# A sparse matmul on one core: one activation tile is loaded on its own, one transposing load is split in two, and a few products change places

## The chip, the cores and the metric

The kernel runs on one NeuronCore of a Trainium2 chip. The metric is the device time of one execution in microseconds (us), lower is better. The time before is 233.01 us, the median of 3 runs that lie between 232.99 and 233.06 us.

## The reference

The weights `w` (1024 x 1024) are pruned 2:4 along the rows: of each four neighbouring rows, per column, the two values with the largest magnitude stay and the others become zero. Then the activations are multiplied by them and a bias is added.

```python
B, S, D = 16, 512, 1024            # bf16 throughout
mag   = jnp.abs(w.reshape(D // 4, 4, D))
order = jnp.argsort(mag, 1)
thr   = jnp.take_along_axis(mag, order[:, 2:3, :], 1)     # the second largest of each four
wp    = (w.reshape(D // 4, 4, D) * (mag >= thr)).reshape(D, D)
return jnp.einsum("bsd,df->bsf", x, wp) + b
```

## The kernel before, in words

The 8192 tokens are 64 tiles of 128 rows. TensorE (PE) computes, for each tile, eight contraction steps of 128 against 1024 output columns in two halves of 512 (h = 0, 1). The weights arrive in two groups of 512 rows (g = 0, 1), and pruning them takes time, so the kernel has a head in which PE works on what is ready already.

**Pieces.** The weights are pruned in six pieces (line 129): pieces 0 to 3 are the four 256-column strips of group 0, pieces 4 and 5 the two 512-column halves of group 1. VectorE (DVE) takes the magnitudes (`abs`), the larger and smaller of each pair (`hi`, `lo`), the threshold (`t1`, `t2`, `thr`), compares (`mask`) and multiplies (`mult`). Each piece has four weight rows of a group, m = 0 to 3, with the letters u, v, s, t; x means u and v together, y means s and t together. The tables `halves` and `part` say in which parts a piece is masked and multiplied, so that a product may begin when its part is there.

**The first seven tiles of x** (0 to 6) are loaded in natural layout, only their first 512 columns (`load_x`, line 102). SyncE (SP) and ScalarE (ACT) each issue loads on a queue of their own. PE transposes these tiles (token `T6a`: four 128x128 transposes of tile 6, line 194), ACT copies the result to SBUF (`C6a`, line 199), and `M6.0t` is the product of tile 6 with row t of piece 0 (128x256, line 224, one matmul; x and y are two). ACT stages finished sums (`S`, `U`, line 259).

**The packed weights** of group 0 and 1 are also copied into natural row order (`spread`, tokens `W0.0`, `W0.1`, `W1.0p`, `W1.0q`, `W1.1`; four copies of 128 KB each, p and q are the first and last two of the four). `W1.0q` is issued by ACT, the rest by SP.

**Tiles 6 to 11** also come by transposing loads into one buffer, `xlead`: `load_lead(0)` at line 128 loads the first 512 columns of tiles 7 to 11, token `X1` (line 354) the last 512 columns of tiles 6 to 11 in a single transposing load. Tokens `Y1` and `Y0` are transposing loads of the last 512 columns of tiles 3 to 5 and 0 to 2 into `xlow` (line 232).

**Products in natural order.** `E0`, `E1` open tile 7 and `A0h0` to `A3h1` open tiles 8 to 11 with the first four contraction steps (line 237). After that the list `closes` gives the last four steps of each half: (8,0), (9,0), (10,0), (11,0), (7,0), (6,0), (3,0), (4,0), (5,0), then (8,1) and so on. They read `xlead`, `xlow` and group 1 of the natural weights; the first one needs all four copies of `W1.0`, (8,1) those of `W1.1`. After the closes, batches of 4 and 8 tiles are loaded whole by transposing loads (`load_nat`, line 396) and multiplied in the same way.

**Order.** The dictionary `order` gives the order of the instructions of PE, DVE, ACT and SP by hand; every engine runs its list strictly in order. `needs` gives the dependencies between tokens, the framework puts the waits in.

Of the kernel before, what the change touches and what calls it, by code (L numbers as in the profile page):

```python
# [10 lines left out]
def kernel(  # L11
# [7 lines left out]
    nc = tc.nc  # L19
    P = 128  # L20
# [14 lines left out]
    HK = D // G  # L35
    assert G == 2 and Dout == 2 * FH and HK == 512
    xf = x.flatten_outer_dims()
    of = out.flatten_outer_dims()

    NPK = 7  # L40
    LEAD = 5
    STG = 8
    SOLO = 6
# [4 lines left out]
    t0 = NPK + LEAD  # L48
# [17 lines left out]
    def seq(eng, inst):  # L66
        if eng in tails:
            tc.add_manual_dep(inst.ins, tails[eng].ins.name, NOSYNC, reason="program order")
        tails[eng] = inst
        return inst  # L70
# [7 lines left out]
    def act(i):  # L78
        return seq("act", i)

    def sp(i):
        return seq("sp", i)
# [12 lines left out]
    def issue(eng, out_, in_):  # L95
        q = nc.sync if eng == "sp" else nc.scalar
        return seq(eng, q.dma_start(out_, in_))  # L97

    def load_w(g, c0, c1, ma=0, mb=4, eng="sp"):
        issue(eng, w_sb[:, g, ma:mb, c0:c1], wv[:, g, ma:mb, c0:c1])  # L100

    def load_x(ta, tb, eng="sp"):
        xs = const.tile([P, tb - ta, HK], bf16, name=f"x_{ta}")
        issue(eng, xs[:], xf[ta * P:tb * P, :HK].rearrange("(t p) k -> p t k", p=P))
        for t in range(ta, tb):
            x_sb[t] = xs[:, t - ta, :]

    xlead = const.tile([P, KT, (LEAD + 1) * P], bf16)

    def load_lead(g):  # L110
        t0 = NPK - g
        sp(nc.sync.dma_start_transpose(out=xlead[:, 4 * g:4 * g + 4, (t0 - SOLO) * P:],
                                       in_=xf[t0 * P:(NPK + LEAD) * P, g * HK:(g + 1) * HK]))
        return {t: xlead[:, :, (t - SOLO) * P:(t - SOLO + 1) * P] for t in range(t0, NPK + LEAD)}

    xnat, held = {}, {}

# [1 line left out]
    load_w(0, 0, 256, 2, 4, "act")  # L119
    load_x(SOLO, SOLO + 1, "act")  # L120
    act(nc.scalar.activation(spark[:], nc.const_aps.tensor(1.0, [P, 1], bf16), Act.Abs))
    load_x(3, 6)
    load_w(0, 256, 512)
    load_x(0, 3)
    load_w(0, 512, 768)
# [9 lines left out]
    def filler(n, rep=1):  # L135
        for _ in range(n):
            pe(nc.tensor.matmul(warm_ps[:, :rep * P], lhsT=nc.const_aps.tensor(1.0, [P, P], bf16),  # L137
                                rhs=nc.const_aps.tensor(1.0, [P, rep * P], bf16), start=True, stop=True))
# [4 lines left out]
    def spread(g, c0, c1, ks=range(4), eng="sp"):  # L143
        for k in ks:
            issue(eng, wp_nat[:, 4 * g + k, c0:c1], wp[32 * k:32 * k + 32, g, :, c0:c1])
# [43 lines left out]
    def transpose(t):  # L189
        xg = x_sb[t].rearrange("p (q m) -> p m q", m=4)  # L190
        bank = psum_o.tile([P, FH], fp32, name="ps") if t in OWN else psum_t.tile([P, FH], fp32, name="tp")
        tp = bank[:].bitcast(bf16)[:, :FH].rearrange("p (m q) -> p m q", m=4)
        for m in range(4):
            pe(nc.tensor.transpose(tp[:, m, :], xg[:, m, :], ident[:]))  # L194
        xpk[t] = tp

    def copy_xt(t):
        xt = xtp.tile([P, 4, P], bf16, name="xt")
        act(nc.scalar.copy(xt[:].bitcast(fp32), xpk[t].bitcast(fp32)))
        xpk[t] = xt  # L200
# [9 lines left out]
    def mm_piece(t, i, ms):  # L210
        g, c0, c1 = pieces[i]
        q, n = pair_of[t], c0 // CW
        if t == SOLO:
            key, d = (t, "h", c0 // FH), -(c0 // FH) * FH
        else:
            key, d = (q, n), pairs[q].index(t) * CW - n * CW
        new = key not in ps_open
        if new:
            ps_open[key] = psum_o.tile([P, FH], fp32, name="ps")
            left[key] = 8  # L220
        ps = ps_open[key]
        for m in range(ms.start, ms.stop):
            left[key] -= 1
            pe(nc.tensor.matmul(ps[:, c0 + d:c1 + d], lhsT=xpk[t][:, m, :],  # L224
                                rhs=wp[:, g, m, c0:c1],
                                start=(new and m == ms.start), stop=(left[key] == 0),
                                skip_group_check=True))

    def load_low(u):
        a, b_ = GROUPS[u]  # L230
        xlow = const.tile([P, 4, (b_ - a) * P], bf16, name=f"xlow{u}")
        sp(nc.sync.dma_start_transpose(out=xlow[:], in_=xf[a * P:b_ * P, HK:]))
        return {a + t: xlow[:, :, t * P:(t + 1) * P] for t in range(b_ - a)}
# [6 lines left out]
    def open_solo(h):  # L240
        ps = ps_open[(NPK, "h", h)] = psum_t.tile([P, FH], fp32, name="tp")
        nat(xnat[NPK], ps[:], h * FH, (h + 1) * FH, 0, 4, last=3)

    def open_nat(j, h):
        t = STG + j
        if j < 3:
            held[(t, h)] = psum_o.tile([P, FH], fp32, name="ps")
        else:
            held[(t, h)] = psum_t.tile([P, FH], fp32, name="tp")
        nat(xnat[t], held[(t, h)][:], h * FH, (h + 1) * FH, 0, 4)  # L250
# [3 lines left out]
    def stage(key):  # L254
        solo = key[1] == "h"
        q, h, at = (pair_of[key[0]], key[2], int(key[0] != SOLO)) if solo else (key[0], key[1] // 2, key[1] % 2)
        if (q, h) not in staged:
            staged[(q, h)] = stg.tile([P, 2, 2, CW], fp32, name="st")
        act(nc.scalar.copy(staged[(q, h)][:, at, :, :].rearrange("p t c -> p (t c)"), ps_open.pop(key)[:]))  # L259

    order = {
# [7 lines left out]
        ),  # L269
        "dve": (  # L270
# [4 lines left out]
        ),  # L275
        "act": (
            "C6a C5a C3a C4a S0b0 C2a C0a C1a abs2 S3b0 S2b0 abs3 S0b1 U6h0 S3b1 S2b1 S0b2 S3b2 S2b2 S0b3 U6h1 "
            "S3b3 S2b3 U7h0 W1.0q U7h1"
        ),
        "sp": (  # L280
            "W0.0 Z W0.1 X1 W1.0p Y1 Y0 W1.1"
        ),
    }
    written = {"X0"}
    p = {}
    halves = {0: tuple("uvst"), 1: ('s', 't', 'x'), 2: ('s', 't', 'x'), 3: ('x', 'y')}

    by_rows = {0}

# [3 lines left out]
    def split_tok(tok):  # L293
        k = tok[-1] if tok[-1] in "xyabuvst" else ""
        return (tok[:-1] if k else tok), k
# [43 lines left out]
    def emit(eng, tok):  # L339
        base, k = split_tok(tok)  # L340
        if tok[0] == "T":
            transpose(int(tok[1:-1]))
            if int(tok[1:-1]) not in OWN:
                transposed.append(tok[1:])
        elif tok[0] == "F":
            filler(int(tok[1:]))
        elif tok[0] == "W":
            g, h = map(int, tok[1:4].split("."))
            spread(g, h * FH, (h + 1) * FH, {"": range(4), "p": range(2), "q": range(2, 4)}[tok[4:]], eng)
        elif tok[0] == "Z":  # L350
            load_w(1, 512, 1024)
            sp(nc.sync.dma_start(bias_sb[:], b.partition_broadcast(P)))
        elif tok[0] == "X":
            xnat.update(load_lead(int(tok[1:])))
        elif tok[0] == "Y":
            xnat.update(load_low(int(tok[1:])))
        elif tok[0] == "E":
            open_solo(int(tok[1:]))
        elif tok[0] == "U":
            t, h = map(int, tok[1:].split("h"))  # L360
            stage((t, "h", h))
        elif tok[0] == "A":
            open_nat(*map(int, tok[1:].split("h")))
        elif tok[0] == "C":
            copy_xt(int(tok[1:-1]))
        elif tok[0] == "M":
            mm_piece(*map(int, base[1:].split(".")), part[k])
        elif tok[0] == "S":
            stage(tuple(map(int, tok[1:].split("b"))))
        else:  # L370
            i = int(base[-1])
            if i not in p:
                p[i] = Piece(i)
            if eng == "act":
                p[i].abs_act()
            else:
                p[i].do(base[:-1], part[k], half.get(k, slice(0, 2)))
# [79 lines left out]
    for bi, (tb, nb) in enumerate(batches):  # L457
        if bi:
            load_batch(bi + 1)
        for j in range(nb):  # L460
            t = tb + j
# [49 lines left out]
```

## Time and profile before

| | |
|---|---|
| median of 3 runs | 233.01 us |
| the profiled execution, its own time | 233.04 us |
| its span, first to last instruction | 231.2 us |
| PE busy | 226.9 us (98%), 1144 matmuls |
| DVE busy | 107.7 us (47%) |
| ACT busy | 14.0 us (6%) |
| POOL busy | 17.6 us (8%) |
| granted TensorE clock over the span | 1.000 |

Times in the rows of the profile count from the start of the span. A row of the timeline has the start in us, the time from its start to the end of the last of its instructions, the engine, the line and operation, the tiles, and how many instructions were merged. Matmuls are pipelined, so one begins before the one ahead has ended: a product of 128x256 lasts 0.27 us by its row, and the next begins 0.109 us after it. SPq and ACTq are the instructions by which SP and ACT issue transfers. A row of the issues has the size in KB and the time from issue to landing.

### The profile page before, as it was taken

The page shows a single profiled execution, that of the slowest core. Times are in us where ns is not written, and L with a number is a line of the kernel's source. Part 1 is how long each engine was busy: PE and PEld are TensorE (multiplying, and loading weights), DVE is VectorE, ACT ScalarE, POOL GpSimd, SP SyncE. Part 2 cuts the span into 40 slices and gives each one's busy share as a digit, 9 for nine tenths or more (in the row PEclk, how much of TensorE's full clock was granted, in tenths as well). Part 3 has the DMA queues.
Part 4 walks back from the last instruction along what each step waited for, and adds up shares of the span by engine and source line. Part 5 has one row for each costly group of instructions (what it writes and reads, how often), then busy time and mean ns, then how long its engine had stood idle before and what let it go on. Part 6 is the DMA issues. An engine that isn't in the chain of part 4 may idle for free.

```text
span 231.2 us, 2827 instructions
## 1 busy us (share of the span) xinstructions
PE 226.9 (98%) x1144; PEld 109.8 (47%) x1144; DVE 107.7 (47%) x194; ACT 14.0 (6%) x27; POOL 17.6 (8%) x15
## 2 busy tenths in 40 slices
PE   7999999999999999999999999999999999999995
PEld 4886444444444444444444444444444444444443
DVE  4999777844424424424424423423423433433434
ACT  2874100000000000000000000000000000000000
POOL 1000299700000000000000000000000000000000
PEclk9999999999999999999999999999999999999999
DMA  6999999997499222991259822797129932122122
GB/s 212 257 200 264 226 191 222 224 323 252 180 218 272 100 94 76 240 274 64 74 124 233 233 91 78 164 208 224 59 91 201 249 140 92 47 91 91 58 81 91
DMA packets 79260, 38.19 MB, mean 165 GB/s; under 512 B 64144, under 2 KB 71696, under 8 KB 79248
## 3 DMA queue, kind: packets, MB, share of 16 engines
q1 hardware_dynamic: 68464, 20.88, 45.8%
q10 hardware_dynamic: 10784, 17.14, 21.3%
q8 instruction: 9, 0.15, 0.3%
q14 instruction: 3, 0.02, 0.0%
HBM read 3.28 MB, written 16.78 MB: 87 GB/s over the span
## 4 chain that ended last, share of the span: by engine, by line
PE 97%; DMA 2%; ACTq 0%; DVE 0%; issue 0%
PE ps L237 88%; PE ps L224 5%; PE tp L237 2%; DMA x<-in_x_dram 2%; PE tp L194 1%; PE ps L194 0%; ACTq L97 0%; DVE o L422 0%
## 5 line engine op out<-in xcount | busy, mean ns | idle before, releaser
L237 PE MATMUL ps<-wp_nat,xb 128*128 128x512 bf16 (+2 forms) x848 | 179.8, 375 | 0.0
L237 PEld LDWEIGHTS <-xb 128*128 128x128 bf16 x848 | 82.4, 98 | 97.5
L422 DVE TENSOR_TENSOR o<-ps,bias_sb 128x512 bf16<-128x512 f32 (+1 forms) x112 | 71.6, 677 | 113.6 <-PE ps L237 113.5
L418 POOL TENSOR_TENSOR st<-st,bias_sb 128x1024 f32<-128x1024 f32 x8 | 16.7, 2125 | 0.0
L237 PE MATMUL ps<-wp_nat,xlead 128*128 128x512 bf16 x64 | 14.9, 379 | 0.0
L237 PEld LDWEIGHTS <-xlead 128*128 128x128 bf16 x88 | 8.6, 98 | 10.3 <-issue 0.3
L224 PE MATMUL ps<-wp,xt 128*128 128x256 bf16 x112 | 12.8, 273 | 0.0
L424 DVE TENSOR_TENSOR o<-ps,st 128x512 bf16<-128x512 f32 x16 | 11.0, 691 | 3.3 <-PE ps L237 2.0
L224 PEld LDWEIGHTS <-xt 128*128 128x128 bf16 x112 | 10.6, 98 | 1.5
L237 PE MATMUL ps<-wp_nat,xlow 128*128 128x512 bf16 x48 | 10.7, 379 | 0.0
L259 ACT COPY st<-ps 128x512 f32<-128x512 f32 x14 | 7.4, 596 | 3.3 <-PE ps L224 3.2
L237 PEld LDWEIGHTS <-xlow 128*128 128x128 bf16 x48 | 4.7, 98 | 5.7
L158 DVE TENSOR_TENSOR mag<-mag,hi 128x256 bf16<-128x256 bf16 (+2 forms) x14 | 6.0, 459 | 0.2
L158 DVE TENSOR_TENSOR wp<-w_sb,mag 128x256 bf16<-128x256 bf16 (+2 forms) x14 | 6.0, 457 | 0.1
L237 PE MATMUL tp<-wp_nat,xlead 128*128 128x512 bf16 x24 | 6.0, 379 | 0.0
L137 PE MATMUL ps<-const-bfloat16-1.0 128*128 128x128 bf16 (+1 forms) x20 | 3.6, 351 | 0.8 <-PEq L495 0.8
L168 DVE TENSOR_SCALAR mag<-w_sb 128x512 uint16<-128x512 uint16 (+2 forms) x5 | 2.3, 476 | 3.3 <-DMA w_sb<-in_w_dram 3.3
L158 DVE TENSOR_TENSOR hi<-mag 128x512 bf16<-128x512 bf16 (+2 forms) x7 | 3.2, 458 | 0.1
L158 DVE TENSOR_TENSOR lo<-mag 128x512 bf16<-128x512 bf16 (+1 forms) x6 | 3.1, 509 | 0.0
L137 PEld LDWEIGHTS <-const-bfloat16-1.0 128*128 128x128 bf16 x20 | 1.8, 118 | 2.4 <-issue 2.4
L194 PEld LDWEIGHTS <-x 128*128 128x128 bf16 x28 | 1.9, 115 | 1.0 <-DMA x<-in_x_dram 0.9
L194 PE MATMUL tp<-ident,x 128*128 128x128 bf16 x16 | 1.5, 223 | 0.8 <-DMA x<-in_x_dram 0.8
(18 smaller groups left out, 16.8 us busy)
## 6 DMA issues: line engine op xcount, KB each, us to landing
out_dram<-o ACTq DMA_DIRECT2D x58, 256.0 KB, 2.4
wp_nat<-wp SPq DMA_DIRECT2D x14, 128.0 KB, 3.7
out_dram<-o ACTq DMA_DIRECT2D x10, 128.0 KB, 1.7
w_sb<-in_w_dram SPq DMA_DIRECT2D x2, 512.0 KB, 5.7
x<-in_x_dram SPq DMA_DIRECT2D x2, 384.0 KB, 4.6
w_sb<-in_w_dram SPq DMA_DIRECT2D x3, 256.0 KB, 5.1
bias_sb<-in_b_dram SPq DMA_DIRECT2D x1, 256.0 KB, 4.5
wp_nat<-wp ACTq DMA_DIRECT2D x2, 128.0 KB, 3.4
```

Of the source, the lines that this page charges most:

```text
L137: pe(nc.tensor.matmul(warm_ps[:, :rep * P], lhsT=nc.const_aps.tensor(1.0, [P, P], bf16), rhs=nc.const_aps.tensor(1.0, [P, rep * P], bf16), ...
L158: dve(nc.vector.tensor_tensor(out, a, b_, op=op))
L168: dve(nc.vector.tensor_single_scalar(self.mag[:, ms, :].bitcast(u16), self.w[:, ms, :].bitcast(u16), 0x7FFF, op=Alu.bitwise_and))
L194: pe(nc.tensor.transpose(tp[:, m, :], xg[:, m, :], ident[:]))
L224: pe(nc.tensor.matmul(ps[:, c0 + d:c1 + d], lhsT=xpk[t][:, m, :], rhs=wp[:, g, m, c0:c1], start=(new and m == ms.start), stop=(left[key] = ...
L237: pe(nc.tensor.matmul(ps, lhsT=xt[:, kt - koff, :], rhs=wp_nat[:, kt, c0:c1], start=(kt == first), stop=(kt == last)))
L259: act(nc.scalar.copy(staged[(q, h)][:, at, :, :].rearrange("p t c -> p (t c)"), ps_open.pop(key)[:]))
L418: pool(nc.gpsimd.tensor_tensor(st[:], st[:], bias.to_broadcast([P, 2, 2, CW]), op=Alu.add))
L422: dve(nc.vector.tensor_tensor(o[:, c0:c1], ps, bias_sb[:, c0:c1], op=Alu.add))
L424: dve(nc.vector.tensor_tensor(o[:, c0:c1].rearrange("p (n c) -> p n c", n=2), ps.rearrange("p (n c) -> p n c", n=2), add, op=Alu.add))
```

## The change

Four things are altered, all of them in the head of the kernel:

- The load of tiles 3, 4 and 5 on SP's queue becomes two: tile 5 alone first, then tiles 3 and 4.
- The second transposing load into `xlead`, tiles 6 to 11, becomes two: `X1` loads tiles 8 to 11, and `X2`, behind `W1.0p` on SP, loads tiles 6 and 7.
- On PE, `M6.0s` trades places with `M5.0t`.
- Piece 3 is masked and multiplied by t, s and x, as pieces 1 and 2 are, in place of x and y, on DVE and in PE's products alike. DVE has six instructions for it where it had four; PE has the same matmuls in another order.

In the changed kernel the transposing loads into `xlead` stand on line 111 in place of 112, lines 123 to 268 keep their numbers, and lines from 270 on are higher by one.

```diff
-    def load_lead(g):
-        t0 = NPK - g
-        sp(nc.sync.dma_start_transpose(out=xlead[:, 4 * g:4 * g + 4, (t0 - SOLO) * P:],
-                                       in_=xf[t0 * P:(NPK + LEAD) * P, g * HK:(g + 1) * HK]))
-        return {t: xlead[:, :, (t - SOLO) * P:(t - SOLO + 1) * P] for t in range(t0, NPK + LEAD)}
+    def load_lead(g, ta=NPK, tb=NPK + LEAD):
+        sp(nc.sync.dma_start_transpose(out=xlead[:, 4 * g:4 * g + 4, (ta - SOLO) * P:(tb - SOLO) * P],
+                                       in_=xf[ta * P:tb * P, g * HK:(g + 1) * HK]))
+        return {t: xlead[:, :, (t - SOLO) * P:(t - SOLO + 1) * P] for t in range(ta, tb)}
...
-    load_x(3, 6)
+    load_x(5, 6)
+    load_x(3, 5)
...
         "pe": (
-            "T6a T5a T3a T4a M6.0t M5.0t M6.0s M5.0s M3.0t ..."
+            "T6a T5a T3a T4a M6.0t M6.0s M5.0t M5.0s M3.0t ..."
...
-            "... M3.3x M4.3x M6.3x M5.3x M2.3x M0.3x M1.3x M3.3y M4.3y M6.3y M5.3y M2.3y M0.3y M1.3y E0 ..."
+            "... M3.3t M4.3t M6.3t M5.3t M2.3t M0.3t M1.3t M3.3s M4.3s M6.3s M5.3s M2.3s M0.3s M1.3s "
+            "M3.3x M4.3x M6.3x M5.3x M2.3x M0.3x M1.3x E0 ..."
...
         "dve": (
-            "... hi3 lo3 t13 t23 thr3 mask3x mask3y mult3x mult3y abs4 ..."
+            "... hi3 lo3 t13 t23 thr3 mask3t mask3s mult3t mask3x mult3s mult3x abs4 ..."
...
         "sp": (
-            "W0.0 Z W0.1 X1 W1.0p Y1 Y0 W1.1"
+            "W0.0 Z W0.1 X1 W1.0p X2 Y1 Y0 W1.1"
...
-    halves = {0: tuple("uvst"), 1: ('s', 't', 'x'), 2: ('s', 't', 'x'), 3: ('x', 'y')}
+    halves = {0: tuple("uvst"), 1: ('s', 't', 'x'), 2: ('s', 't', 'x'), 3: ('s', 't', 'x')}
...
         elif tok[0] == "X":
-            xnat.update(load_lead(int(tok[1:])))
+            xnat.update(load_lead(1, *((STG, NPK + LEAD) if tok == "X1" else (SOLO, STG))))
```

11 rows, old and new, of the table order are left out of this document.

## The prediction

> **What bounds the kernel now.** I read the page first, for the share of PE, then the chain of waits, for the places where PE doesn't run on without a break.
>
> ```profile
> PE 226.9 (98%) x1144; PEld 109.8 (47%) x1144; DVE 107.7 (47%) x194; ACT 14.0 (6%) x27; POOL 17.6 (8%) x15
> ```
>
> ```profile
> 1.27 3.85 DMA x<-in_x_dram
> ```
>
> ```profile
> 5.16 0.74 PE tp L194 x8
> 5.90 0.45 PE ps L194 x8
> ```
>
> ```profile
> 24.53 2.59 PE ps L237 x12
> ```
>
> ```profile
> 27.98 2.72 PE ps L237 x12
> ```
>
> The chain waits for a load of x until 5.11 and is on PE from 5.16 to the end. So only time that PE loses can be won, and the change touches nothing behind the last product from `xlow`, at 48.5 by a row below. After 5.16 the losses are small: twelve matmuls take 2.59 us in one place and 2.72 us from 27.98, so 0.13 us is lost there. The timeline of PE, looked at in narrow windows, shows that place and two more.
>
> ```profile
> 5.16 0.41 PE L194 MATMUL tp<-ident,x 128*128 128x128 bf16 x4 [0.77 <-DMA x<-in_x_dram]
> ```
>
> ```profile
> 5.48 0.41 PE L194 MATMUL tp<-ident,x 128*128 128x128 bf16 x4
> ```
>
> ```profile
> 6.18 0.47 PE L224 MATMUL ps<-wp,xt 128*128 128x256 bf16 x2
> ```
>
> ```profile
> 6.37 0.50 PE L224 MATMUL ps<-wp,xt 128*128 128x256 bf16 x3
> ```
>
> ```profile
> 27.82 0.73 PE L237 MATMUL ps<-wp_nat,xlead 128*128 128x512 bf16 x2
> ```
>
> T6a's four transposes begin at 5.16 and T5a's at 5.48. The last eight transposes, from 5.90, take 0.45 us, 0.056 each, so T5a could begin at 5.38, or 5.41 with some 0.03 for starting after a wait: 0.07 us lost, and 0.03 more for T5a's own start. M6.0t begins at 6.18 and the next product at 6.37, where products step by 0.11 (the three from 6.37 to 6.87 last 0.27 each): 0.08 lost. At 27.82 two matmuls take 0.73 us; one lasts 0.38 (a row below has 379 ns), so the second began at 28.17, 0.35 behind the first in place of 0.22: the 0.13 again. All of it is some 0.3 us. **That is the ceiling of this change**, 0.13% of the span.
>
> **The head, part by part.** What arrives when is told by the issues and their times to landing, one stretch each.
>
> ```profile
> x<-in_x_dram SPq DMA_DIRECT2D x1, 384.0 KB, 4.2
> w_sb<-in_w_dram SPq DMA_DIRECT2D x1, 256.0 KB, 4.5
> x<-in_x_dram ACTq DMA_DIRECT2D x1, 128.0 KB, 3.8
> ```
>
> ```profile
> x<-in_x_dram SPq DMA_DIRECT2D x1, 384.0 KB, 4.9
> ```
>
> ```profile
> 1.24 0.46 SPq L97 DMA_DIRECT2D x<-in_x_dram  x1
> 1.75 0.68 SPq L97 DMA_DIRECT2D w_sb<-in_w_dram  x1
> 2.47 0.61 SPq L97 DMA_DIRECT2D x<-in_x_dram  x1
> ```
>
> ```profile
> 5.20 6.44 SPq L112 DMA_TRANSPOSE xlead<-in_x_dram  x1
> ```
>
> ```profile
> 19.17 4.02 SPq L112 DMA_TRANSPOSE xlead<-in_x_dram  x1
> ```
>
> Tile 6, on ACT's queue, lands at 1.27 + 3.8 = 5.1 and starts PE; nothing of the change moves it forward. Tiles 3 to 5 land at 1.24 + 4.2 = 5.44, piece 1's weights at 1.75 + 4.5 = 6.25, tiles 0 to 2 at 2.47 + 4.9 = 7.4. *Tile 5 alone* is a third of that load, of tile 6's size and issued at the same 1.24, so it should land with tile 6 or before it; I take no wait at T5a. Tiles 3 and 4 are issued 0.51 us later, which is the step from one SP issue to the next (1.24 to 1.75), and so is all that follows on SP up to `load_lead(0)`. These landings are paced by bytes, though: 256 KB lands 0.81 us behind the 384 KB, the next 384 KB 1.1 us behind that, 320 to 350 KB each us, while each had been issued over 3 us before the one ahead of it had landed. An issue later by 0.51 still comes before its turn, so the landings stay: 5.44 for tiles 3 and 4, wanted by T3a at 5.16 + 8 x 0.056 + 0.03 = 5.64. I cost the added issue at nothing; without that cover it is 0.51 us on each load, which is the second rival.
>
> PE then ends the sixteen transposes at 5.16 + 16 x 0.056 + 0.03 = 6.08, not 6.18. Now the products want their operands.
>
> ```profile
> 5.93 0.38 ACT L199 COPY xt<-tp 128x256 f32<-128x256 f32 x1
> ```
>
> ```profile
> 5.93 0.28 DVE L158 TENSOR_TENSOR wp<-w_sb,mag 128x256 bf16<-128x256 bf16 x1
> ```
>
> C5a ends at 5.93 + 0.38 = 6.31 and the product behind it starts at 6.37: 0.06 us from end to use. `mult0s` ends at 5.93 + 0.28 = 6.21, `mult0t` one step of DVE ahead of it; DVE's work isn't touched there. So M6.0t may begin at 6.08, *M6.0s* (in M5.0t's place) at 6.21 + 0.06 = 6.27, and the third product, M5.0t, at 6.38; C5a, started by its transposes 0.05 earlier, is done by then. In before the third product begins at 6.37 + 0.11 = 6.48. **The head gains 0.10 us**, not the sum of its gaps, since `mult0s` is late next. T2a follows 0.10 earlier too:
>
> ```profile
> 7.80 0.39 PE L194 MATMUL tp<-ident,x 128*128 128x128 bf16 x4
> ```
>
> That is 7.70, with its first weights loaded 0.1 before; tiles 0 to 2 have landed by 7.4.
>
> *Piece 3 by t, s, x.* Two rows of before, one of each form, give its price.
>
> ```profile
> 14.93 0.76 DVE L158 TENSOR_TENSOR mag<-mag,hi 128x512 bf16<-128x512 bf16 x2
> 15.60 0.76 DVE L158 TENSOR_TENSOR wp<-w_sb,mag 128x512 bf16<-128x512 bf16 x2
> 16.27 0.69 DVE L168 TENSOR_SCALAR mag<-w_sb 128x2048 uint16<-128x2048 uint16 x1
> ```
>
> ```profile
> 11.92 0.49 DVE L158 TENSOR_TENSOR mag<-mag,hi 128x256 bf16<-128x256 bf16 x2
> ```
>
> ```profile
> 13.41 0.42 DVE L158 TENSOR_TENSOR hi<-mag 128x512 bf16<-128x512 bf16 x1
> ```
>
> ```profile
> 15.91 0.49 PE L224 MATMUL ps<-wp,xt 128*128 128x256 bf16 x3
> ```
>
> The old form lasts 16.27 - 14.93 = 1.34 us, the new one, as piece 2 has it, 13.41 - 11.92 = 1.49. DVE is later by 0.15 from there on. Piece 3's first product is the last of the row from 15.91 (15.91 + 2 x 0.11 = 16.13); its `mult3x` ended at 15.60 + 0.42 = 16.02, so with PE 0.10 earlier it would have just been waited for, some 0.05. In the new form `mult3t` is done at about 15.6, `mult3s` is wanted 0.76 later, x at 17.6, and all are there. It wins nothing now, and keeps what the head won.
>
> **The split of X1.** What PE waited for at 27.82 isn't named by the view of waits. The second matmul of that stretch needs the second copy of `W1.0p`:
>
> ```profile
> 23.96 0.89 SPq L97 DMA_DIRECT2D wp_nat<-wp  x1
> ```
>
> ```profile
> wp_nat<-wp SPq DMA_DIRECT2D x1, 128.0 KB, 4.2
> xlow<-in_x_dram SPq DMA_TRANSPOSE x1, 5.1
> ```
>
> ```profile
> 20.84 1.22 DVE L158 TENSOR_TENSOR wp<-w_sb,mag 128x2048 bf16<-128x2048 bf16 x1
> ```
>
> It lands at 23.96 + 4.2 = 28.16, and the matmul starts at 28.17. Its issue stood behind `X1`, which held SP from 19.17 for 4.02 us, while its weights (`mult4`) were done at 22.06. With four of six tiles `X1` holds SP for an estimated 4.02 x 4/6 = 2.7 us, to 21.85, or 22.35 if the 0.51 of the head is still there; `mult4`, later by 0.15, ends at 22.21. So `W1.0p` is issued about 0.9 to 1.1 us earlier, lands near 27.1, and PE, 0.10 earlier, wants it at 27.94. **0.13 us goes**, with 0.8 to spare. `X1` itself, shorter, lands before its 19.17 + 6.6 = 25.8 of now.
>
> `X2` is put behind, and its price on SP is estimated from the next rows: `Y1` holds SP for 1.81 us with 3 tiles, so 2 tiles are 1.2 us.
>
> ```profile
> xlead<-in_x_dram SPq DMA_TRANSPOSE x1, 6.6
> ```
>
> ```profile
> 24.90 1.81 SPq L232 DMA_TRANSPOSE xlow<-in_x_dram  x1
> ```
>
> ```profile
> wp_nat<-wp SPq DMA_DIRECT2D x1, 128.0 KB, 3.6
> ```
>
> ```profile
> 31.02 1.33 SPq L97 DMA_DIRECT2D wp_nat<-wp  x1
> ```
>
> ```profile
> L237 PE MATMUL ps<-wp_nat,xlow x48: 379/379/379, 33.1 to 48.5; 128*128 128x512 bf16 x48
> ```
>
> ```profile
> 35.73 1.46 PE L237 MATMUL ps<-wp_nat,xlead 128*128 128x512 bf16 x6
> ```
>
> Tile 7 is wanted at 27.82 + 16 x 0.216 + 0.13 = 31.4; `X2`, issued near 24.0 and landing in the 5.1 to 6.6 us of its kind, is there by 30.6 at worst. What is queued behind it is `Y1`, `Y0` and `W1.1`. `W1.1`'s last copy was issued at 31.02 and landed 3.6 later at 34.65; its first user is the fourth matmul from 35.73, at 36.38: 1.7 us of slack. The two splits nearly cancel on SP (1.3 less, 1.2 more, at most 0.5 from the head), so that slack holds. `Y1`, landed at 24.90 + 5.1 = 30.0 and first used at 33.1, has 3 us.
>
> **The sum.** 233.04 (the profiled execution: 231.2 of span and 1.8 around it, which stay) - 0.10 - 0.13 = **232.80 us**. The median is 233.01, 0.03 below this execution; I make no correction for it.
>
> **Rivals.** (1) *Only the second gain comes.* Tile 5 lands no earlier, or `mult0s` is used later than 0.06 behind its end: 233.04 - 0.13 = 232.91. For it: tile 6, issued with tile 5 and as large, landed only at 5.1. Chance 0.11.
>
> (2) *The added issue delays the loads.* If tiles 3 and 4 land 0.51 later, at 5.95, T3a waits from 5.64, M6.0t begins near 6.43 and all is 0.25 later than before; 0.13 comes back at 28: 233.16. Against it stands the pacing by bytes above. The Trainium skill, "DMA: Bandwidth & Descriptors", section "Rules for kernel authors", speaks for it: many small transfers are to be coalesced into one large one. By the fixed 2.0 us for one DMA of its section "Anatomy of one DMA", there for transfers that GpSimd issues, tiles 3 and 4 would be 1.8 us late at T3a, an estimate of 234.6 us. The trace disagrees that such a cost adds up in a queue: the landings follow each other by 0.8 to 1.1 us. Chance 0.08.
>
> (3) *Nothing is gained.* `W1.0p`'s second copy has a transposing load behind it in both kernels, and its landing took 4.2 us where that of the last copy of `W1.1` took 3.6. If its landing hangs on something other than its issue, PE waits until 28.17 again, and what the head won is lost in the same wait: 233.04. Chance 0.10.
>
> (4) *Slower: transposing loads don't cost by tiles.* The load of 5 tiles held SP for 6.44 us, that of 6 tiles for 4.02, `Y1` with 3 for 1.81. If `X1` still holds SP for 4 us and `X2` comes on top with 1.2 (as `Y1`) to 2.6 us (2 x 6.44 / 5), `W1.0p` isn't earlier, and `W1.1` moves back by that and the 0.5 of the head, up to 3.1 us. It costs nothing up to 1.7 us and all that is over it: up to 1.4 us, 233.04 to 234.4; I take 233.6. Against it: the 6.44 fell while earlier loads were still landing (the transposing load was issued at 5.20, tiles 0 to 2 landed at 7.4 and two weight loads of 256 KB each come behind them). Chance 0.12.
>
> **How the numbers follow.** Forecast 0.56, (1) 0.11, (2) 0.08, (3) 0.10, (4) 0.12, and 0.03 for a gain that I don't see. Below 232.57 or above 233.48, 0.2%, is about what a measurement of this kernel can tell from no change: the forecast, (1), (2) and (3) all lie within, so same 0.85; (4) is slower, 0.12; faster 0.03. The range goes from the ceiling of the gaps, 233.04 - 0.31, with 0.08 for the run's own spread, 232.65, up to rival (2) with a little over, 233.2, and leaves out (4).
>
> **What would show it.** Right: T5a follows T6a without a gap, the third product starts near 6.38, T2a near 7.70, `W1.0p`'s second copy is issued before 23.1, and the twelve matmuls behind 27.7 take 2.59 us. Wrong: a wait of PE at T3a or T2a (rival 2), the second copy still landing after 28 (3), or PE idle near 36 before (8,1) (4). A time under 232.6 would mean that PE lost time in before where I saw none.

## The result and the profile after

The changed kernel takes **233.36 us**, the median of 15 runs (233.11 to 233.89); the kernel before, run beside it, 233.06 (15 runs). The ratio is 1.0015, with a 95% interval of 1.0008 to 1.0021: slower, by some 0.3 us. The forecast was 232.80, with a range up to 233.2, so the time lies outside. The profiled execution took 233.36 us, with a span of 231.6 (233.04 and 231.2 in before).

The chain of waits of the changed kernel (start, length, what) runs through another load of x than that of before: not tile 6, with which PE begins, but tiles 0 to 2, for which it stops once more. Three of its pieces:

```profile
2.93 5.41 DMA x<-in_x_dram
...
8.38 0.41 PE tp L194 x4
...
28.57 2.59 PE ps L237 x12
```

The twelve matmuls that took 2.72 us from 27.98 take 2.59 here: the wait of 0.13 near 28 isn't there. What came on top is a wait for tiles 0 to 2, issued at 2.93 and landed at 8.34. The rows of PE's timeline in the head show it:

```profile
4.78 0.98 PE L194 MATMUL tp<-ident,x 128*128 128x128 bf16 x8
5.60 0.61 PE L194 MATMUL ps<-ident,x 128*128 128x128 bf16 x8
6.28 1.78 PE L224 MATMUL ps<-wp,xt 128*128 128x256 bf16 x14
8.38 0.41 PE L194 MATMUL tp<-ident,x 128*128 128x128 bf16 x4 [0.33 <-DMA x<-in_x_dram]
```

The gap between T6a and T5a is closed, as the change means it, yet the first product begins at 6.28 (6.18 in before), and T2a at 8.38 in place of 7.80. That is 0.58 late, of which 0.10 is the later first product; less the 0.13 near 28 it makes 0.45, and the span grew by 0.4. The rest of the head keeps pace.

Where the wait comes from is read from the issues (KB, us to landing) and from two stretches of the head: start and end, length, busy time of PE, PE's weight loads, DVE, ACT and POOL, the granted clock, the DMA's share and GB/s. First the issues of the changed kernel:

```profile
x<-in_x_dram SPq DMA_DIRECT2D x1, 384.0 KB, 5.4
x<-in_x_dram SPq DMA_DIRECT2D x1, 256.0 KB, 3.7
...
x<-in_x_dram SPq DMA_DIRECT2D x1, 128.0 KB, 2.8
x<-in_x_dram ACTq DMA_DIRECT2D x1, 128.0 KB, 3.1
```

The same two stretches of before:

```profile
2.00:4.40 2.40, 2.39 (x18) 1.36 (x16) 1.10 (x5) 1.28 (x2) 0.00 (x0) 1.00 1.03 320
4.40:7.40 3.00, 2.24 (x27) 1.83 (x28) 2.90 (x14) 1.25 (x4) 0.00 (x0) 1.00 1.09 319
```

and of the changed kernel:

```profile
2.00:4.40 2.40, 2.40 (x15) 1.57 (x14) 0.94 (x4) 1.27 (x2) 0.00 (x0) 1.00 0.98 300
4.40:7.40 3.00, 2.93 (x32) 2.61 (x30) 2.93 (x14) 1.27 (x4) 0.00 (x0) 1.00 0.97 289
```

Tile 5 does land early, at 1.24 + 2.8 = 4.0, and tile 6 at 4.4, 0.7 ahead of before. But from 2.0 to 7.4 us the transfers move 2.4 x 300 + 3.0 x 289 = 1587 KB, where they moved 2.4 x 320 + 3.0 x 319 = 1725 KB (of 1000 bytes here, of 1024 in the rows of the issues). The 138 KB that are missing are 0.43 us at 320 GB/s. Tiles 3 and 4 (5.49) and piece 1's weights (6.27) still land as forecast; of the loads that PE waits for in the head, tiles 0 to 2 alone are late. Each load is spread over sixteen DMA engines and has landed when the last of them has; in before the sixteen parts of tiles 0 to 2 landed between 6.75 and 7.41, in the changed kernel the first also at 6.76 and thirteen by 7.29, but the fourteenth at 7.99 and the last at 8.34. So it is three parts that are late, and not the load as a whole.

### The profile page after: what moved, and what is told of

Its sections match the earlier page's. It is cut to its first block, busy times and chain, and to the rows that moved or that the text cites. A ratio compares the mean times of both kernels' runs of the same rounds, so it can differ in the third digit from the quotient of the medians.

```text
span 231.6 us, 2831 instructions
## 1 busy us (share of the span) xinstructions
PE 227.7 (98%) x1144; PEld 110.8 (48%) x1144; DVE 108.1 (47%) x196; ACT 14.1 (6%) x27; POOL 17.6 (8%) x15
## 4 chain that ended last, share of the span: by engine, by line
PE 95%; DMA 2%; SPq 1%; issue 0%; DVE 0%
PE ps L237 88%; PE ps L224 5%; DMA x<-in_x_dram 2%; PE tp L237 2%; SPq L97 1%; PE tp L194 0%; DVE o L423 0%; PE ps L194 0%
## 5 line engine op out<-in xcount | busy, mean ns | idle before, releaser
L137 PE MATMUL ps<-const-bfloat16-1.0 128*128 128x128 bf16 (+1 forms) x20 | 4.2, 408 | 0.8 <-PEq L496 0.8
L408 POOL COPY pruned<-wp 128x1 bf16<-128x1 bf16 x1 | 0.2, 187 | 27.1 <-DVE wp L158 27.1
```

Source lines behind the costliest of these rows:

```text
L408: pool(nc.gpsimd.tensor_copy(out=pruned[:], in_=wp[:, 1, 3, Dout - 1:]))
```

## The experiments

Each was timed beside the kernel before; the times quoted are medians, the ratios come with their 95% intervals. "Uncut" means that tiles 3 to 5 come in one load. The expectations stand as they were written ahead of the runs. A landing told without a row is the last of a load's sixteen parts in the trace.

**Which part of the change costs.** The changed kernel with tiles 3 to 5 in one load again:

```diff
-    load_x(5, 6)
-    load_x(3, 5)
+    load_x(3, 6)
```

> The changed kernel with tiles 3 to 5 in one load again. Theory A (the extra load on SP's queue pushes the load of tiles 0 to 2 back and PE waits for it at T2a): the gains stay and the loss goes, T2a near 7.8 at the latest and the end 0.1 to 0.25 us below the kernel before. Rival B (the late landing in the one profile is chance, and the loss comes from the split of X1 or from the order of the products): 0.2 to 0.4 us above the kernel before, as the changed kernel.

Measured: 233.01 us against 233.10, ratio 0.9992 [0.9980, 1.0004]. The loss is gone with the cut, but the gain of 0.1 to 0.25 isn't shown. Near 28 the chain of this kernel has no wait:

```profile
28.38 2.59 PE ps L236 x12
```

In the head its profiled execution, at 233.21 above its median, did not do as expected: T2a begins at 8.19 and not by 7.8.

```profile
5.75 0.92 PE L193 MATMUL ps<-ident,x 128*128 128x128 bf16 x8
6.50 1.69 PE L223 MATMUL ps<-wp,xt 128*128 128x256 bf16 x14
8.19 0.41 PE L193 MATMUL tp<-ident,x 128*128 128x128 bf16 x4
```

Tiles 0 to 2 landed at 8.14 here too, and the products began only at 6.50, since the transposes ahead of them were slow: eight from 5.75 to 6.50, 0.094 us each. With fourteen products of 0.109, T2a would have begun at 8.03 without the late landing. One execution is thus no measure of the cut; what tells it apart is the medians.

The kernel before with this cut alone:

```diff
-    load_x(3, 6)
+    load_x(5, 6)
+    load_x(3, 5)
```

> The kernel before with tile 5 loaded alone and nothing else changed. Theory A: tiles 0 to 2 land near 8.3 us, T2a waits, and the end is 0.3 to 0.5 us above the kernel before. Rival B: within 0.1 us of the kernel before or a little below it.

Measured: 233.61 us, +0.51, ratio 1.0023 [1.0011, 1.0035]. In the profiled execution T3a waits, tiles 3 and 4 having landed at 6.05:

```profile
6.10 0.64 PE L195 MATMUL ps<-ident,x 128*128 128x128 bf16 x8 [0.94 <-DMA x<-in_x_dram]
```

and PE waits once more near 28, since the unsplit `X1` comes later on SP and `W1.0p` behind it:

```profile
28.16 0.38 PE L238 MATMUL ps<-wp_nat,xlead 128*128 128x512 bf16 x1
29.03 1.24 PE L238 MATMUL ps<-wp_nat,xlead 128*128 128x512 bf16 x5 [0.49 <-DMA wp_nat<-wp]
```

The second matmul of the group could have begun at 28.16 + 0.22 = 28.38 and begins at 29.03, 0.65 late.

With the rest of the change the cut cost 0.30, by itself 0.51; so the split of `X1` may be worth more behind the cut than alone, but the two intervals overlap. The next run is before with `X1` and `X2` split alone:

```diff
...
-            "W0.0 Z W0.1 X1 W1.0p Y1 Y0 W1.1"
+            "W0.0 Z W0.1 X1 W1.0p X2 Y1 Y0 W1.1"
...
-            xnat.update(load_lead(int(tok[1:])))
+            xnat.update(load_lead(1, *((STG, NPK + LEAD) if tok == "X1" else (SOLO, STG))))
```

> The kernel before with X1 split in X1 and X2 and nothing else. Theory A: the wait near 28 us goes, 0.1 to 0.15 us below the kernel before. Rival B, if the split is to blame: 0.2 to 0.4 us above it, with a PE gap behind 28 us.

Measured: 233.01, -0.09, ratio 0.9994 [0.9984, 1.0004]: of the size of the 0.13, but not outside the scatter. And before with the order rows alone (`M6.0s` ahead of `M5.0t`, piece 3 by t, s, x):

```diff
-            "T6a T5a T3a T4a M6.0t M5.0t M6.0s M5.0s M3.0t ..."
+            "T6a T5a T3a T4a M6.0t M6.0s M5.0t M5.0s M3.0t ..."
...
-    halves = {0: tuple("uvst"), 1: ('s', 't', 'x'), 2: ('s', 't', 'x'), 3: ('x', 'y')}
+    halves = {0: tuple("uvst"), 1: ('s', 't', 'x'), 2: ('s', 't', 'x'), 3: ('s', 't', 'x')}
```

> The kernel before with only the order of the products and piece 3 by t, s, x. Theory A: the 0.08 us won at the third product is lost again in the wait near 28 us, so the same within 0.1 us. Rival B, if the order is to blame: 0.2 to 0.4 us above it.

Measured: 233.07, -0.03, ratio 0.9998 [0.9987, 1.0009]. Neither gain nor loss. **The loss comes with the cut of the load:** there with it in both kernels, and gone without it.

**Is it the added issue?** A load of 2 KB that nothing reads, put into before on SP behind tiles 3 to 5, adds the same step to SP without cutting anything.

```diff
     load_x(3, 6)
+    scratch = const.tile([P, 8], bf16, name="scratch")
+    issue("sp", scratch[:], b.rearrange("(p k) -> p k", p=P))
     load_w(0, 256, 512)
```

> The kernel before with one load of 2 KB more on SP's queue, between tiles 3 to 5 and piece 1's weights, whose data nobody reads; no load of x is split. Theory A: 0.3 to 0.5 us above the kernel before, with tiles 0 to 2 landing later and T2a waiting. Rival C: within 0.1 us of it.

Measured: 232.96 against 233.03, ratio 1.0001 [0.9992, 1.0010]. SP's timeline shows all the loads behind it 0.51 us later:

```profile
1.75 0.48 SPq L97 DMA_DIRECT2D scratch<-in_b_dram  x1
2.27 0.66 SPq L97 DMA_DIRECT2D w_sb<-in_w_dram  x1
2.98 0.61 SPq L97 DMA_DIRECT2D x<-in_x_dram  x1
```

and PE's shows that T2a is on time; tiles 0 to 2 landed at 7.38 (7.41 in before):

```profile
7.82 0.39 PE L196 MATMUL tp<-ident,x 128*128 128x128 bf16 x4
```

The same load behind tiles 0 to 2:

```diff
     load_x(0, 3)
+    scratch = const.tile([P, 8], bf16, name="scratch")
+    issue("sp", scratch[:], b.rearrange("(p k) -> p k", p=P))
```

> The same load of 2 KB, but behind tiles 0 to 2 on SP's queue, so that only the later weights and SP's later list are moved back. Theory A in the form that the loss is at T2a: within 0.1 us of the kernel before. If it is SP's later list (X1 and W1.0p behind it) that loses: 0.2 to 0.5 us above it, with a longer wait of PE near 28 us.

Measured: 232.95, ratio 0.9998 [0.9989, 1.0006]. A later issue by itself costs nothing that these runs can tell: the second rival, as it was put, falls.

These two kernels have `X1` whole, and should have the wait near 28. The chain of the first of them hasn't, nor has that of the second (28.11, 2.59):

```profile
28.12 2.59 PE ps L239 x12
```

In these executions `X1` held SP for 3.67 and 3.52 us, not 4.02, and the second copy of `W1.0p` landed at 27.50 and 26.76, not after 28.

**Is it SP's queue, or the order in it?** Tile 5 moved to ACT's queue, behind tile 6:

```diff
     load_x(SOLO, SOLO + 1, "act")
+    load_x(5, 6, "act")
...
-    load_x(5, 6)
     load_x(3, 5)
```

> The changed kernel, but tile 5 is loaded alone on ACT's queue behind tile 6, so that SP's queue has no issue more than before. Theory A (the added issue on SP, 0.48 us, makes the loads behind it late): the loss goes, 0 to 0.2 us below the kernel before. Rival C (the split itself costs, wherever it is issued, since one more load shares the engines): 0.2 to 0.4 us above it.

Measured: 233.18, ratio 1.0018 [0.9999, 1.0038]: some of the loss may stay, but the interval just covers 1. The profiled execution (234.09) lies 0.9 above this median; in it tile 5 landed at 6.75:

```profile
6.79 0.41 PE L194 MATMUL tp<-ident,x 128*128 128x128 bf16 x4 [1.21 <-DMA x<-in_x_dram]
```

Tiles 0 to 2 moved ahead of piece 1's weights, with the cut kept:

```diff
-    load_w(0, 256, 512)
     load_x(0, 3)
+    load_w(0, 256, 512)
```

> The changed kernel with the load of tiles 0 to 2 ahead of piece 1's weights on SP's queue. If the loss is PE's wait at T2a: tiles 0 to 2 land near 6.5 to 7, T2a doesn't wait, and the end falls to 0.1 us above to 0.2 us below the kernel before, unless piece 1's weights, now landing near 7.5, hold DVE and M3.1t by more than the 0.4 us they have. If the loss is elsewhere: 0.3 us above as it is.

Measured: 234.33, +1.30, ratio 1.0062 [1.0045, 1.0078]. It doesn't help: tiles 3 and 4, which stand ahead of the exchange, landed at 7.02 and held T3a up.

```profile
7.06 0.64 PE L194 MATMUL ps<-ident,x 128*128 128x128 bf16 x8 [1.52 <-DMA x<-in_x_dram]
```

Tiles 3 and 4 first, then tile 5:

```diff
-    load_x(5, 6)
     load_x(3, 5)
+    load_x(5, 6)
```

> The changed kernel with tiles 3 and 4 loaded first and tile 5 behind them, so the same two loads in the other order; T5a then waits for all three tiles, as before the change. Theory C (cutting the load of three tiles in two costs, whichever part is first: the second part's packets begin late and long, and every load behind it on the same engines with them): 0.3 to 0.6 us above the kernel before, the second part landing at 5.5 to 7. Rival H (tile 5 alone ahead competes with tile 6, two loads of one tile at once on two queues): within 0.15 us of the kernel before.

Measured: 233.20, +0.18, ratio 1.0005 [0.9996, 1.0015], not told apart from no change, and between the two expectations. One by one, 5, 3, 4:

```diff
     load_x(5, 6)
-    load_x(3, 5)
+    load_x(3, 4)
+    load_x(4, 5)
```

> The changed kernel with tiles 5, 3 and 4 loaded one by one, so the suspected cut twice. Theory C: 0.6 to 1.0 us above the kernel before. Rival H, and an issue that costs nothing (as the load of 2 KB showed): 0.2 to 0.4 us, as the changed kernel.

Measured: 233.61, +0.59, ratio 1.0025 [1.0016, 1.0033]. Tiles 5 and 6 as one load of 256 KB on ACT, 3 and 4 on SP, so that there are as many loads of x as in before:

```diff
-    load_x(SOLO, SOLO + 1, "act")
+    load_x(5, 7, "act")
...
-    load_x(5, 6)
     load_x(3, 5)
```

> The changed kernel with tiles 5 and 6 in one load of 256 KB on ACT's queue and tiles 3 and 4 on SP's, so as many loads of x as before the change. Theory C in the form that the number of loads counts: 0 to 0.25 us below the kernel before. If any cut of the load of three tiles costs, whatever is joined in its place: 0.2 us or more above it.

Measured: 233.02 against 233.02, ratio 1.0000 [0.9991, 1.0008]. All on SP, tile 6 first, then tile 5, then 3 and 4:

```diff
-    load_x(SOLO, SOLO + 1, "act")
...
+    load_x(SOLO, SOLO + 1)
     load_x(5, 6)
     load_x(3, 5)
```

> The changed kernel with tile 6 moved to SP's queue, ahead of tile 5, so that no two loads of x are under way on two queues at once; one more issue on SP, which costs little. Rival H (two queues compete): the loss goes, within 0.15 us of the kernel before or below. Theory C: 0.3 to 0.6 us above it.

Measured: 234.22, +1.20, ratio 1.0041 [1.0027, 1.0055]. With no load of x on a second queue the loss is larger; that two loads of x on two queues disturb each other is not needed for it. The stretches show how little is moved, 2.4 x 209 + 3.0 x 254 = 1264 KB:

```profile
2.00:4.40 2.40, 2.40 (x19) 1.55 (x18) 0.91 (x4) 0.75 (x2) 0.00 (x0) 1.00 0.80 209
4.40:7.40 3.00, 2.04 (x26) 1.49 (x24) 2.76 (x13) 1.39 (x4) 0.00 (x0) 1.00 0.95 254
```

**Any cut, or this one?** Up to here every loss came with a load of x cut at the head of SP's queue, but the runs did not say whether cutting, one-tile loads or the place is what costs. Three kernels, all with the rest of the change, cut something else. Tile 2 off the load of tiles 0 to 2:

```diff
-    load_x(5, 6)
-    load_x(3, 5)
+    load_x(3, 6)
     load_w(0, 256, 512)
-    load_x(0, 3)
+    load_x(2, 3)
+    load_x(0, 2)
```

> The changed kernel with tiles 3 to 5 in one load again, and tile 2 cut off the load of tiles 0 to 2 instead, in front of it. Theory C (any one-tile load put into SP's queue puts some of the sixteen DMA engines behind): tiles 0 and 1 land 8.2 or later, T2a is at its time of the uncut kernel (7.8 to 8.2) or later, the time is 0.2 to 0.5 above the kernel before. Rival D (only a cut of the queue's first load of x costs, since the loads behind it inherit the delay): tile 2 lands early, by 7.4, T2a begins at 7.4 to 7.8, tiles 0 and 1 are there when wanted, time within 0.1 of the kernel before or below.

Measured: **232.89 us** against 233.06, ratio 0.9988 [0.9979, 0.9998], the only kernel of the sixteen here whose interval lies below 1. A one-tile load in SP's queue is no harm there, and with four loads of x, as in the changed kernel, their number isn't what costs. That cutting tile 2 off gains anything is not shown: the kernel has the rest of the change as well, which without any cut of x is at -0.09 (above) and -0.19 (next). PE's timeline has T6a and T5a almost without a gap and T2a on time:

```profile
4.93 0.68 PE L194 MATMUL tp<-ident,x 128*128 128x128 bf16 x8 [0.59 <-DMA x<-in_x_dram]
5.45 0.61 PE L194 MATMUL ps<-ident,x 128*128 128x128 bf16 x8
6.19 1.78 PE L224 MATMUL ps<-wp,xt 128*128 128x256 bf16 x14
7.81 0.39 PE L194 MATMUL tp<-ident,x 128*128 128x128 bf16 x4
```

and there is no wait in the group near 28 either:

```profile
28.00 2.59 PE ps L237 x12
```

Piece 1's weights in two loads of 128 KB:

```diff
-    load_x(5, 6)
-    load_x(3, 5)
-    load_w(0, 256, 512)
+    load_x(3, 6)
+    load_w(0, 256, 512, 2, 4)
+    load_w(0, 256, 512, 0, 2)
```

> The changed kernel with tiles 3 to 5 in one load again, and piece 1's weights, 256 KB, cut into rows s and t and then rows u and v, 128 KB each. One issue more ahead of tiles 0 to 2, and two loads of 128 KB of weights. Theory C in its wide form (every cut of a load into parts of 128 KB costs): tiles 0 to 2 land at 8.2 to 8.6, T2a waits until 8.2 or later, the time is 0.2 to 0.5 above the kernel before. Rival E (only a cut of the loads of x does it, by the rows that they read from): T2a as in the uncut kernel, 7.8 to 8.2, time within 0.1 of the kernel before.

Measured: 232.87, -0.19, ratio 0.9993 [0.9984, 1.0001]. No loss either. And the load of tiles 3 to 5 cut across the partitions, 192 KB each:

```diff
-    load_x(5, 6)
-    load_x(3, 5)
+    xs = const.tile([P, 3, HK], bf16, name="x_3")
+    xv = xf[3 * P:6 * P, :HK].rearrange("(t p) k -> p t k", p=P)
+    issue("sp", xs[:64], xv[:64])
+    issue("sp", xs[64:], xv[64:])
+    for t in range(3, 6):
+        x_sb[t] = xs[:, t - 3, :]
```

> The changed kernel with the load of tiles 3 to 5 cut across the partitions in place of the tiles: two loads of 192 KB, each with three tiles for 64 partitions. The same number of loads as the changed kernel, and no one-tile load on SP; tile 5 comes with the others. If the number of loads costs: T3a or T2a is late as in the changed kernel, T2a at 8.2 to 8.6, 0.2 to 0.5 above the kernel before. If it is the one-tile load of 128 KB alone ahead: T2a at 7.8 to 8.2, time within 0.1 of the kernel before.

Measured: 234.14, +1.08, ratio 1.0051 [1.0033, 1.0068]. Its second half landed at 6.53, and now tile 5 needs it:

```profile
6.66 0.39 PE L198 MATMUL tp<-ident,x 128*128 128x128 bf16 x4 [1.25 <-DMA x<-in_x_dram]
```

```profile
2.00:4.40 2.40, 2.40 (x15) 1.57 (x14) 0.89 (x4) 1.29 (x2) 0.00 (x0) 1.00 0.93 269
4.40:7.40 3.00, 1.75 (x23) 1.52 (x22) 2.93 (x14) 0.69 (x3) 0.00 (x0) 1.00 1.04 259
```

Here no load of x on SP has a single tile, and the bytes moved fall to 2.4 x 269 + 3.0 x 259 = 1423 KB all the same. The Trainium skill, "DMA: Bandwidth & Descriptors", section "Rules for kernel authors", says that two transfers to disjoint halves of the partitions are not worth making, and one of all 128 is to be used. This run agrees, with +1.08 us.

All runs side by side, in the order of the bytes; the KB are worked out from the two stretches as above, T2a is its start, both from the one profiled execution; the last two columns are from all runs.

| kernel | first load of x on SP, KB | KB from 2.0 to 7.4 us | T2a, us | median against before, us | ratio, 95% interval |
|---|---|---|---|---|---|
| tile 2 cut off | 384 | 1726 | 7.81 | -0.17 | 0.9979 to 0.9998 |
| before | 384 | 1725 | 7.80 | | |
| piece 1's weights cut | 384 | 1718 | 7.91 | -0.19 | 0.9984 to 1.0001 |
| 2 KB load early | 384 | 1699 | 7.82 | -0.07 | 0.9992 to 1.0010 |
| uncut | 384 | 1689 | 8.19 | -0.09 | 0.9980 to 1.0004 |
| 2 KB load late | 384 | 1685 | 7.91 | -0.08 | 0.9989 to 1.0006 |
| only `X1`, `X2` | 384 | 1646 | 7.84 | -0.09 | 0.9984 to 1.0004 |
| tiles 5, 6 in one on ACT | 256 | 1643 | 7.89 | 0.00 | 0.9991 to 1.0008 |
| one by one | 128 | 1634 | 8.28 | +0.59 | 1.0016 to 1.0033 |
| tiles 3, 4 first | 256 | 1595 | 8.11 | +0.18 | 0.9996 to 1.0015 |
| **the changed kernel** | 128 | 1587 | 8.38 | +0.30 | 1.0008 to 1.0021 |
| only the order rows | 384 | 1587 | 8.11 | -0.03 | 0.9987 to 1.0009 |
| only the cut | 128 | 1540 | 8.14 | +0.51 | 1.0011 to 1.0035 |
| tile 5 on ACT | 256 | 1533 | 9.10 | +0.15 | 0.9999 to 1.0038 |
| tiles 0 to 2 earlier | 128 | 1463 | 9.10 | +1.30 | 1.0045 to 1.0078 |
| cut across partitions | 192 | 1423 | 8.95 | +1.08 | 1.0033 to 1.0068 |
| all on SP | 128 | 1264 | 9.70 | +1.20 | 1.0027 to 1.0055 |

The second column sorts the medians, a pattern that was seen after the runs: with 384 KB first all seven lie at -0.19 to -0.03, with 256 KB at 0.00 to +0.18, with 128 or 192 KB at +0.30 to +1.30. Where PE waits in the profiles differs: for tiles 0 to 2 at T2a in the changed kernel, one by one, tiles 3 and 4 first and all on SP; already at T3a or T5a in only the cut, tile 5 on ACT, tiles 0 to 2 earlier and the cut across partitions. The profiled executions follow the column less strictly: the kernel with only the order rows moved 1587 KB in its profile, as the changed kernel did, and landed tiles 0 to 2 at 8.06, yet its median is that of no change. Such an execution happens without the cut; that it is the usual one with it is inferred from the medians, as each kernel has one profile.

## Why the prediction was wrong, point by point

**The head's loads: the step that failed.** "An issue later by 0.51 still comes before its turn, so the landings stay: 5.44 for tiles 3 and 4 ... I cost the added issue at nothing." The first half holds: with the 2 KB load, tiles 0 to 2 were issued 0.51 later and landed on time. What failed is "the landings stay": in the changed kernel they do for tiles 3 and 4 (5.49 for 5.44), but not for tiles 0 to 2, which were to have landed by 7.4; with the cut alone tiles 3 and 4 are late too (6.05). I took the pace of 320 to 350 KB each us for a constant of the machine that any cut of the same bytes would keep. In the changed kernel tiles 0 to 2 landed at 8.34, which is 384 KB in 8.34 - 6.27 = 2.07 us behind the weights, 186 KB each us. I had priced the cut by its instruction on SP alone, and not by what it does to the transfers; T2a had 7.80 - 7.41 = 0.39 us of cover; the landing, 8.34 - 7.41 = 0.93 later, took that and 0.54 more, and PE began 0.04 behind it.

**Tile 5 by itself.** Right: landed by 4.0, no wait at T5a. It won nothing, as the next point shows.

**The head's gain of 0.10.** It didn't come, and would not have come reliably. M6.0t was to begin at 6.08, for which `mult0t` had to be done by 6.01 as in before. DVE's rows, of before and of the changed kernel:

```profile
5.73 0.49 DVE L158 TENSOR_TENSOR wp<-w_sb,mag 128x256 bf16<-128x256 bf16 x2
5.93 0.49 DVE L158 TENSOR_TENSOR wp<-w_sb,mag 128x256 bf16<-128x256 bf16 x2
```

The second begins 0.20 later, because the second half of piece 0's weights landed at 3.70 and not at 3.50. M6.0t then begins at 6.28. In the kernel with tile 2 cut off that landing was 3.63 and M6.0t at 6.19. From before's profile I read DVE's times as fixed, though they hang on a landing that varied from 3.44 to 3.75 over the profiled executions of this study; a head gain of 0.10 is smaller than that. The transposes vary too. I priced all sixteen at the 0.056 of before; in the changed kernel the first eight took 0.10 each, and in three profiles (uncut, only the order rows, one by one) so many were slow that the products began at 6.49 to 6.50.

**Piece 3 by t, s, x** costs nothing: right, as far as the run of the order rows alone can tell (-0.03).

**The split of X1.** Right in its mechanism and its times, not in its gain. SP's timeline in the changed kernel, with the issue of the second copy of `W1.0p`, the later of the two from 22.74, once more in a row of its own:

```profile
19.98 2.19 SPq L111 DMA_TRANSPOSE xlead<-in_x_dram  x1
22.74 1.20 SPq L97 DMA_DIRECT2D wp_nat<-wp  x2
23.34 0.60 SPq L97 DMA_DIRECT2D wp_nat<-wp  x1
23.98 1.44 SPq L111 DMA_TRANSPOSE xlead<-in_x_dram  x1
```

`X1` holds SP for 2.19 us (2.7 estimated), `X2` for 1.44 (1.2), and the copy is issued at 23.34, somewhat behind the 23.1 that I named, and landed at 26.88 (27.1). No profile of a kernel with the split has a wait near 28. But of the four without it that kept tiles 3 to 5 in one load, three don't wait there either (the two with the 2 KB load, and the order rows alone, whose group from 28.30 takes 2.59): the 0.13 belonged to the one execution that I had, in which `X1` held SP longest of the four. The split pays where that load falls badly: with the cut alone, `X1` whole held SP for 4.67 us and the wait was 0.65. In the medians it is worth some 0.1, if anything (-0.09 alone, interval across 1). `W1.1` still came in time, but with less to spare than the 1.7 us that I gave it: its last copy landed at 36.18, and its first user is the fourth matmul of

```profile
36.18 1.67 PE L237 MATMUL ps<-wp_nat,xlead 128*128 128x512 bf16 x7
```

at 36.18 + 3 x 0.216 = 36.83, so 0.65 us. The fourth rival didn't happen.

**The sum.** For the two profiled executions -0.10 became +0.58, and 0.13 went: 233.04 + 0.58 - 0.13 = 233.49, where 233.36 was measured and the spans differ by 0.4. In medians the cut costs 0.39 (+0.30 with it, -0.09 without). Both gains together, 0.23 in the forecast, are 0.09 to 0.19 in the three kernels that have the rest of the change and tiles 3 to 5 in one load (-0.09, -0.17, -0.19), two of whose intervals cross 1.

**The rivals.** The second one had the right sign, a landing late behind the cut, but priced it at T3a, where the changed kernel doesn't wait; T2a it named among the signs alone. Its price hung on the 0.51 of the issue, which the 2 KB load showed to be free, so its 233.16 had the wrong reason, and that it lies within 0.2 of the time measured is luck. The sentence on coalescing from the Trainium skill, "DMA: Bandwidth & Descriptors", section "Rules for kernel authors", pointed the right way for the first load of x, though not for the loads behind it, whose cuts cost nothing; the fixed cost for each DMA that I worked out beside it did not, as the 2 KB loads are DMAs too, and cost nothing. Of the first rival the missing head gain came true, with `mult0t` late and not the causes that it names; the third's sign, the second copy landing after 28, didn't come (26.88).

**What stays open.** Why the kernels with a smaller first load of x on SP's queue lose time. The runs show that the loss comes with the cut. The profiles show that the transfers then mostly move fewer bytes until 7.4 us, and in the changed kernel that three of the sixteen parts of tiles 0 to 2 end late. They don't show what holds these up, and the trace doesn't tell one engine's packets from another's. The place in the queue and the size of the first load were not varied apart from each other in more than the cases above, and a first load of more than 384 KB wasn't tried.

## What to carry to other kernels

Cost a load that is cut by what it does to all the loads that follow in its queue, down to the last one that an engine waits for, and not by its issue: here an issue more was free, and the cut cost 0.39 us, in the changed kernel through a load three places behind. The same cut can be free elsewhere: tile 2 off the second load of x on SP, in place of tile 5 off the first, brought no loss (232.89 against 233.06). And when a gain of 0.1 us hangs on landings, look at how much the landings vary before counting it.

## What the runs showed of the hardware that was not expected

- The same 384 KB as 128 + 256 KB, 192 + 192 KB or 3 x 128 KB, as the first load of x on SP's queue, cost 0.30 to 1.08 us; as 256 + 128 KB it wasn't told apart from no change (+0.18). 384 KB as 128 + 256 KB further back, or 256 KB of weights as 2 x 128 KB, cost nothing.
- The parts of one load of x on the sixteen DMA engines landed up to 2.2 us apart (as tiles 3 and 4, issued before tiles 0 to 2 in the kernel with these moved ahead: 4.83 to 7.02), where 0.66 us is what before had for both its large loads of x.
- PE's transposes ran at two steps in the head. In the changed kernel T6a's and T5a's eight take 5.60 - 4.78 = 0.82 us, 0.10 each; in the kernel with tile 2 cut off they take 0.52, which less 0.03 for each of two starts after a wait is 0.06 each. The granted clock reads 1.00 in both. By the starts of the single transposes the steps are 0.107 and 0.056, and the change from one to the other comes near 3.6 us in before, while PE still runs the matmuls on constants ahead of T6a, near 5.5 in the changed kernel and near 6.4 in the uncut one. Beginning at 4.78 in place of 5.16, PE won nothing by it, as M6.0t waited for `mult0t`. The Trainium skill, "TensorE: Matmul & The Clock Gate", section "Part 1: The HAM clock gate", says that PE runs at half rate until a window of about 3.4 us, which runs free of the kernel, has been busy, so that the change comes at another time in each execution; its steps for 128 columns are 0.107 and 0.056. The two steps and the varying time of the change agree with it; the window itself no run here shows, and the granted clock of the rows doesn't show the change.
